# Lag products for two channels at once, both products of a table step in one instruction, and a new order: a gated mix of memory attention and a state-space convolution

## The chip, the cores and the metric

One core of one Trainium2 chip runs the whole program. Time is in device microseconds of that core. Before the change three runs gave 304.19, 305.31 and 306.17 us; the median is 305.31. Tables and prices below come from one profiled execution of the same kernel.

The engines are TensorE (PE, with its weight loads shown apart as PEld), VectorE (DVE), ScalarE (ACT), GpSimd (POOL) and SyncE (SP), which issues the DMAs.

## What is computed

A sequence x of 2048 tokens with 512 channels goes through two branches that a per-token gate mixes:

```python
g = sigmoid((x * gate_w).sum(-1, keepdims=True))
a = A_ref(x, wq, wk, wv, wo, beta)     # 32 heads of 16, 4 segments of 512 tokens
b = B_ref(x, A_re, A_im, B_re, B_im, C_re, C_im, log_dt, Dskip)
out = g * a + (1 - g) * b
```

Branch A is attention inside each segment (scores, causal mask, softmax, product with v) and, from the second segment on, a memory read: phi(q) times a matrix M, divided by phi(q) times z, where M and z gather phi(k) and v of the segments before. The two are mixed per head and projected with wo.

Branch B is a long convolution per channel d:

```python
dt = exp(log_dt)[:, None]
P  = exp((dt * A)[:, :, None] * l)           # d x 128 x l, l in bf16
K  = einsum('dn,dnl,dn->dl', C, P, dt * B).real
y  = irfft(rfft(pad(u)) * rfft(pad(K)))[:, :L] + u * Dskip
```

The lags l are rounded to bf16, so only some 640 distinct lags occur among the 2048. Each of them is a sum f + g of one of 20 exponents and one of 32. For one channel, K at all these lags is the real part of a product of two small complex matrices over n = 128: a table G of 32 entries (C times dt B, times a power) and a table F of 20 entries (powers of exp(dt A)).

## The kernel before, in words

The program is a graph of 1779 operations, built in Python by `build_graph`. Each has an engine (or may be done by ACT or DVE, for evacuations of PSUM), its operands and the tiles it needs. `ORDER` (line 370) is one long string with all the operations by number, in the order in which they enter their engines' queues: a suffix a or v puts an evacuation on ACT or DVE, and the numbers behind slashes name the buffers taken. `replay` reads it, `emit` (line 264) turns dependences into semaphore waits. On DVE and ACT these cover operations of the same engine too; on PE they do not. So within each engine the instructions run strictly as `ORDER` has them. The `cost` arguments and the `S.key` times belong to the search that made the string and do nothing on the chip.

The work falls into parts that overlap in time.

- Preparation (`ssm_prep`, line 754): six parameter matrices are transposed on PE two at a time (line 763) and evacuated (line 768); dt comes from a one-row matmul and an exponential on ACT (line 774); then sines, cosines and exponentials give exp(dt A). `ssm_powers` (line 816) squares it nine times, on ACT (826) and DVE (827, 828), and writes each power to a `pw` tile in bf16. `ssm_cb` makes C times dt B in `CBT` and a diagonal term.
- Attention: for 4 segments and 4 groups of 8 heads, projections, scores, one exponential of 128x2048 on ACT (line 1100, 80 in all), products with v, normalisation on DVE (lines 1072 to 1075), memory read, transpose to `oT`.
- Tables (`tables`, line 1169): for each of four blocks of 128 channels, 12 calls of `cmul` fill the tiles F and G. In a tile, the partition is n and the free index is channel pair, entry, channel within the pair; the real plane of 64 pairs comes first and the imaginary one behind it. A `cmul` step multiplies n entries by one power: a product with the real part, written in place (line 1197), a product with the imaginary part into a scratch tile `t2` (line 1200), and an addition of `t2` with its planes exchanged (line 1204).
- Lag products (line 1234): for each channel, the G table (32 columns, taken as PE's weights) times the F table (20 columns), first one plane, then the other. Four channels sit side by side in four column tiles of 32. A block takes 256 matmuls in 8 groups of 32, two evacuations of 320 columns into `kex`, and four DMAs that spread `kex` over the partitions of `KTT`.
- Convolution (`conv`, line 1251): x goes through a first transform (`x_level1`, line 876) and by way of DRAM (`scr_Z`); 32 steps transform K and x, multiply on DVE (line 1328), transform back and write `V2`. The constants `c_DN` are loaded step by step.
- The last part (`finals`) sums all into 16 output tiles and stores them.

F, G and the pool of `t2` (two buffers) lie at the same addresses as the buffers of the convolution's second half. In the trace nearly all matmuls carry one line (696, a helper), and evacuations carry lines 226 and 227 (ACT and DVE) or 229 and 230 (with a scale); DMAs carry line 222.

Of the kernel before, what the change touches and what calls it, by code (L numbers as in the profile page):

```python
# [98 lines left out]
class Sched:  # L99
# [45 lines left out]
    def ap(self, T, off=0, dims=None, p0=0, np_=128, n=None, dt=None, pstep=1):  # L145
        dt = dt or T.dt
        T = T.tile
        esz = 4 if dt == F32 else 2
        if T.isp:
            h = self.ps32 if dt == F32 else self.ps16  # L150
            base = T.slot * 2048 // esz
        else:
            h = self.sb32 if dt == F32 else self.sb16
            base = (T.pool.addr + T.slot * T.pool.size) // esz
        v = h[:]
        st = v.ap[0][0]
        if dims is None:
            dims = [[1, n]]
        return bass.AP(v.tensor, v.offset + p0 * st + base + off, [[pstep * st, np_]] + [list(d) for d in dims])

# [210 lines left out]
10/0 0/0 9/1 29/4/0 15/0 16/0 35/0/0 36 214/0 30v 45/0 46/1 27/0 198/0 37/2 38/3 40/4 44/5 41 47/6 63/0 66/1 42 48  # L371
64/2 39/7 51/0 13/2 43 53/8 49 50 14/3 67v/0 52/9 56/0 54/10 55 70/1 58/11 57/12 61/0 59/13 60 68/0 69 76/2 82/3
33/5/1 65a 83v/0 22/0 3/0 80/1 26/0 81 17/3 18 11/4 12/5 31/0/2 32v 199 62 94/4 23/0 71v/1 95v/2 92/2 93 209/1/0/0
210a 84 187/5 400/1 74/3 24/0 7/0 75 1/0 211 107v/3 72 106/6 221/2 182/7 223/0/0/0 96 386/0 34a 104/0 105 212/6/0 222a
262/7/1 215/1 185/1 213a 224 263a 108 118/1 188/2 186/0 86/3 116/0 808/0 217/2 73 1003v/0 225 200 85 1004v 97 117
190/1 87/0 249/0/0 216a 131v/4 218a 19 250 251 130/3 88 20 1223/1 226 259/1/1/1 128/0 183/3 260a 261 387/2 129 809/0
810/0 388 5/0 1244/0 142/4 109 1005v 184 228/0/1 229 132 264/1/1/1 230 597/0 140/0 141 143v/5 219/0 205/2 119a/6 154/5
237/0/2 238 120 265 266 1007a/0 1012/0 1011 1009/1 1006a 201/0 21 1013 403/1 152/3 239 206 153 8/0 164/0 1008 267
207/0 1224/3/0 1225a 220a 598/2 121 167v/7 1017 599 98/3 2/0 1010 232/0/3 233 1018/0 234 168 1014 1019 165/1 231/2 166
1015/1 302/3/2/2 155v/8 1226/0 133 1016 1020 100/7 176a/9 1227a 144 275/0/1 276 235 236 99 404a 202/0 1021/0 277 177  # L380
169 1026 1022 1027/1 303a 244/0 240 305/1/2 241/1 6/0 156 306a 245/0/3 1028 246 247 4/0 145 1024/0 1245/3/1 343/1/0/0
344a 1246a 208/0 189 242 110/0 304 1247/1 1248a 1023 178 1029 1228 1236/3/0 280/0/2 281 157 248 345 1249 1237a 282 252
1234/1 1030/1 1235a 1238 1032 1231/3/1 1025 1232a 253 243/0 271/0/3 272 273 346/1/0 1031 1229/3 1033/0 1230a 347a
292/0/0 1039/1 1034 1255/2/0 293 1256a 111/6 294 1233 1038 274/3 1239/1/1 254/2 112 255 1035 1257/2 278 1258a 1240a
288/0/3 289 279 290 389 1040 227/2/0 268 1241/1 1242a 256 283 284/3 307/0/0/0 308 390/0 269/0 1259 316/0/1 317 318
1042/0 1036/1 287/2 291 1243 1041 285 1265/1 257/1 258a/0 1043 122/3 295 296 329/0/2 310 330 1037 331 297/4 203 191
1044/1/0 309 123/3 1045 1046 298 124 286/1 1047 1048a 204 136/5 299 348/0/1/1 391/1 349 134/2 312/0/3 313 314 270 135
1049/1 350 1250/3/0 1251a 1050 1051 1052 1053a 1054/0 1057 1055 146/0 1252/2 1253a 333/0/0 334 335 1254 1062v/0 315/0
1061v/0 392/3/1/1 1059v 393a 1058v 1056 148/4 1060v 1283/1/1 1284a 1067/0 28/0 1066 319 320 1063 1064/1 1068 1065 1072
1260/2/0 1073/0 113v/1 1082/1 355/0/3 356 1074 452/3/1 114 147 311/1 351 352 1069 1075 115 357 89a/3 1076/0 1081  # L390
321/0/1 322 1077 453a 353 90 1261a 323 91 407/3 408a 158/1 1078 328/2 324 325/5 1083 326 409/1/0/0 410 411 1262/3
1263a 1085/0 359/0/1 360 1079/1 327/0 101a/0 102 361 1084 405/3 499/1/2/2 406a 332 500a 125a/6 1087 364/0/2 365 366
1080 192/0 193/0 126 401/3 336 337 1086 338/0 394 1286/0 1088/1 339 1281/1 1282a 1264 402a 1094/0 1089 372/0/0 373
1271/0/0 374 1272a 103 1093 137a/4 395/1/2 396a 358/3 362 340 363 376/0/3 377 371/0 127 378 367 1095 1273/2 1274a 1285
160/1 449/1/0/0 450a 414/0/1 1090 1091/1 415 1070/0 375 379 457/2/1/1 1275 416 458 1092 300/1 301a 368/1 1097/1 77a/7
1096 1071 418/0/2 369 419 1098 459 380 381/2 420 1104/1/1 149v/5 78 1105 159 79 501 451 1106 1107 138 139 382 383/1
161a/8 1268/2/1 431/0/0 173v/2 432 170/3 172/7 370 171 433 1108v 616/0/0 174 175 456/0 179v/9 1269a 1099/3 1100 1101
1102 1117a/0 1113a/0 435/0/3 1103a 617a 1111 1292/1/0 412 1116v 1115v 436 1293a 1114v 162 1118 1119/0 1122/1 502/2/0
1121 437 1120 163 1266/3 1294/0 417/1 1123 1128/0 180 421 1267a 1270 1124 1127 150 151 423/0/1 424 1137/1 460 503a
# [1077 lines left out]
```

## Time and profile before

| | us |
|---|---|
| median of three runs | 305.31 |
| the profiled execution, whole | 304.8 |
| its span, first to last instruction | 303.0 |
| first of the 80 score exponentials starts | 22.0 |
| last of them ends | 278.1 |
| products and additions of the tables (lines 1197 to 1204) | 28.9 to about 161 |
| busy time of lines 1197, 1200, 1204 | 33.6, 33.5, 32.5 |
| busy time of the 1024 lag matmuls | 10.1 |
| mean granted clock | 0.974 |

The 1.8 us between span and whole lie outside the instructions. Busy time of a group is the union of its instructions, and the mean of one, in ns, stands behind it. Instructions on DVE and ACT overlap: the next one starts before the last has ended, so the step from start to start is shorter than the duration. The chain of waits is followed back from the last instruction; a piece called issue is time in which an engine waited for nothing that the profile shows. A stretch's row gives each engine's busy time in it with the number of instructions.

### The profile page before, as it was taken

The numbers are of one execution on the slowest core, as the hardware profiler recorded it, in microseconds if no ns is written. First come the engines' busy times: TensorE is split into PE (matmuls) and PEld (weight loads), VectorE is DVE, ScalarE is ACT, GpSimd is POOL, SyncE is SP. The second block draws the span as 40 slices with busy tenths as digits, with TensorE's granted clock in tenths as the row PEclk, the third lists the DMA queues.
The fourth block names the chain that finished last, engine by engine and source line by source line (L and its number), as shares of the span: only waits on it lengthen the run. The fifth ranks groups of instructions, "written<-read, shape, count | busy, mean of one in ns | idle before, by whom it ended". The sixth has DMA issues, their size and how long they took to land.

```text
span 303.0 us, 9760 instructions
## 1 busy us (share of the span) xinstructions
PE 263.9 (87%) x4154; PEld 155.4 (51%) x4154; DVE 263.4 (87%) x630; ACT 262.8 (87%) x327; POOL 3.2 (1%) x9
## 2 busy tenths in 40 slices
PE   2798767787877979889997999989999999999993
PEld 1544435554554625575753666555545455545651
DVE  2999999999999899799997799999999998856182
ACT  2999999999998997999997999998889899888121
POOL 2000000000000000000000000000000000000000
PEclk9999999999988978999998999999999999999998
DMA  6989122322401333234520256676586665730234
GB/s 151 270 177 204 41 90 98 114 59 44 134 35 43 110 125 106 82 112 141 142 74 4 66 150 191 182 209 188 167 238 180 185 202 159 249 107 2 69 116 163
DMA packets 46589, 39.23 MB, mean 129 GB/s; under 512 B 21585, under 2 KB 42450, under 8 KB 46546
## 3 DMA queue, kind: packets, MB, share of 16 engines
q1 hardware_dynamic: 46546, 38.60, 45.1%
q8 instruction: 33, 0.54, 0.7%
q14 instruction: 10, 0.08, 0.1%
HBM read 20.37 MB, written 6.29 MB: 88 GB/s over the span
## 4 chain that ended last, share of the span: by engine, by line
PE 44%; DVE 27%; ACT 19%; issue 4%; DMA 3%; SPq 1%; DVEq 0%
PE psum L696 43%; ACT sb L1100 9%; DVE sb L1200 7%; DVE sb L1197 7%; DVE sb L1204 6%; ACT sb L226 5%; ACT sb L826 2%; DMA sb<-c_DN 2%; SPq L222 1%; DMA sb<-sb 1%; DMA sb<-in_B_A_re_dram 1%; DVE sb L1075 1%; DVE sb L1022 1%; DVE sb L1154 1%; DVE sb L1072 1%
## 5 line engine op out<-in xcount | busy, mean ns | idle before, releaser
L696 PE MATMUL psum<-sb 128*128 128x17 bf16 (+12 forms) x4066 | 258.0, 229 | 27.1 <-ACT sb L1100 12.7
L696 PEld LDWEIGHTS psum<-sb 128*128 128x128 bf16 (+4 forms) x4066 | 149.4, 96 | 133.3 <-ACT sb L1100 26.9
L1100 ACT ACTIVATE sb<-psum 128x2048 bf16<-128x2048 f32 x80 | 152.2, 1902 | 7.4 <-PE psum L696 6.8
L226 ACT ACTIVATE sb<-psum 128x512 bf16<-128x512 f32 (+3 forms) x156 | 86.0, 608 | 13.1 <-PE psum L696 12.7
L227 DVE CAST sb<-psum 128x512 bf16<-128x512 f32 (+2 forms) x58 | 35.9, 629 | 5.5 <-PE psum L696 4.9
L1197 DVE TENSOR_TENSOR sb<-sb 128x512 bf16<-128x512 bf16 (+3 forms) x48 | 33.6, 717 | 0.3 <-ACT sb L226 0.2
L1200 DVE TENSOR_TENSOR sb<-sb 128x512 bf16<-128x512 bf16 (+3 forms) x48 | 33.5, 712 | 0.1
L1204 DVE TENSOR_TENSOR sb<-sb 128x512 bf16<-128x512 bf16 (+3 forms) x48 | 32.5, 687 | 0.2
L1112 DVE TENSOR_TENSOR sb<-sb 128x1024 bf16<-128x1024 bf16 (+1 forms) x40 | 23.0, 577 | 3.5 <-ACT sb L1100 3.4
L1328 DVE TENSOR_TENSOR sb<-sb 128x1024 bf16<-128x1024 bf16 x32 | 21.7, 684 | 2.8 <-DMA sb<-sb 2.5
L229 ACT ACTIVATE sb<-psum,sb 128x512 f32<-128x512 f32 (+1 forms) x11 | 7.1, 685 | 9.1 <-PE psum L696 9.0
L1075 DVE TENSOR_TENSOR sb<-psum,sb 128x256 bf16<-128x256 f32 x32 | 13.4, 418 | 0.4
L1072 DVE RECIPROCAL sb<-psum 128x16 f32<-128x16 f32 x32 | 8.0, 252 | 4.8 <-PE psum L696 4.6
L826 ACT ACTIVATE sb<-sb 128x512 f32<-128x512 f32 x18 | 11.7, 658 | 0.0
L230 DVE TENSOR_SCALAR sb<-psum,sb 128x512 bf16<-128x512 f32 (+1 forms) x5 | 3.7, 748 | 6.4 <-PE psum L696 6.4
L1154 DVE TENSOR_TENSOR sb<-psum,sb 128x512 bf16<-128x512 f32 x12 | 8.2, 688 | 0.3
L1031 ACT ACTIVATE sb<-sb 128x512 bf16<-128x512 bf16 x12 | 7.6, 637 | 0.3 <-PE psum L696 0.3
L827 DVE TENSOR_TENSOR sb<-sb 128x256 f32<-128x256 f32 x18 | 7.6, 422 | 0.0
L980 ACT ACTIVATE sb<-psum 128x512 bf16<-128x512 bf16 x12 | 7.6, 634 | 0.0
L828 DVE SCALAR_TENSOR_TENSOR sb<-sb 128x256 f32<-128x256 f32 x18 | 7.4, 419 | 0.0
L1385 DVE SCALAR_TENSOR_TENSOR sb<-psum,sb 128x512 bf16<-128x512 f32 x8 | 5.6, 745 | 1.3 <-PE psum L696 1.2
L763 PE MATMUL psum<-sb 128*128 128x128 bf16 x24 | 2.7, 280 | 4.4 <-DMA sb<-in_B_A_re_dram 4.4
(70 smaller groups left out, 105.8 us busy)
## 6 DMA issues: line engine op xcount, KB each, us to landing
sb<-sb SPq DMA_DIRECT2D x64, 128.0 KB, 3.2
sb<-c_DN SPq DMA_DIRECT2D x32, 224.0 KB, 2.9
scr_Z<-sb SPq DMA_DIRECT2D x16, 256.0 KB, 2.1
sb<-scr_Z SPq DMA_DIRECT2D x16, 256.0 KB, 3.8
sb<-in_A_x_dram SPq DMA_DIRECT2D x5, 512.0 KB, 4.5
out_dram<-sb SPq DMA_DIRECT2D x8, 256.0 KB, 2.3
sb<-c_DN SPq DMA_DIRECT2D x12, 160.0 KB, 2.3
sb<-sb SPq DMA_DIRECT2D x20, 64.0 KB, 2.0
```

The lines of the kernel that those rows point to most:

```text
L226: fa = lambda e: e.activation(dst(), src(), ACT.Copy)
L227: fd = lambda e: e.tensor_copy(dst(), src())
L696: mm = lambda e, o_, l, r_, st, sp, **kw: e.matmul(o_, lhsT=l, rhs=r_, start=st, stop=sp, skip_group_check=True, **kw)
L826: op("ACT", ("As", 512), lambda e, sq=sq, Z=Z: e.activation(ap(sq, n=512), ap(Z, n=512), ACT.Square), r=[Z], w=[sq], key=PW[h] + PWS * k)
L1075: op("DVE", ("V1", 256), lambda e: e.tensor_tensor(ap(o1, gi * 16, [[128, 4], [32, 4], [1, 16]]), ap(T, dims=[[68, 4], [17, 4], [1, 16]]), ...
L1100: o = op("ACT", ("Ax", 2048), lambda e, P=P, pT=pT: e.activation(ap(pT, n=2048), ap(P, n=2048), ACT.Exp, scale=0.25), r=[P], w=[pT])
L1112: op("DVE", ("V2", 128 * nb), lambda e, pT=pT, dims=dims: e.tensor_tensor(ap(pT, dims=dims + [[1, 128]]), ap(pT, dims=dims + [[1, 128]]), ...
L1154: op("DVE", ("V1", 512), lambda e: e.tensor_tensor(ap(o2, 0, [[128, 4], [16, 8], [1, 16]]), ap(P2, 0, [[256, 4], [17, 8], [1, 16]]), ap(R2 ...
L1197: op("DVE", ("V2n1" if n == 1 else "V2", 256 * n), lambda e: e.tensor_tensor(run(tile, ne, dst, 1), run(tile, ne, src, sstep), ap(pw, cl * ...
L1200: op("DVE", ("V2n1" if n == 1 else "V2", 256 * n), lambda e: e.tensor_tensor(run(t2, n, 0, 1), run(tile, ne, src, sstep), ap(pw, cl * 512 ...
L1204: op("DVE", ("V2n1" if n == 1 else "V2", 256 * n), lambda e: e.tensor_tensor(D_(), D_(), ap(t2, n * 128, [[-n * 128, 2], [2 * n, 64], [1, ...
L1328: op("DVE", ("V2", 1024), lambda e, Y=Y, XAB=XAB, K3=K3, xo=xo: e.tensor_tensor(ap(Y, dims=[[512, 2], [1, 512]]), ap(XAB, xo, [[512, 2], [ ...
```

## The change

It has five parts.

1. F and G grow by spare entries behind the real ones: 4 for F (20 become 24) and 8 for G (32 become 40). The tile `t2` goes. A `cmul` step whose source entries are adjacent writes both products in one instruction with an outer dimension of two: real to the destination, imaginary to the spare entries. Three of the twelve steps of a table (sources 5, 2 and 2 entries apart) keep two instructions. The addition reads the spare entries. 27 instructions per table instead of 36.
2. A lag matmul takes a pair of channels: 64 weight columns (32 entries of each) by 40 columns (20 of each), in two column tiles of 64. Half of the 64 by 40 results mix the two channels and are not used. 128 matmuls per block, in 8 groups of 16; three evacuations (480, 480 and 320 columns) into a `kex` of twice the size with one buffer.
3. So that the right rows come out, channels are permuted: channel c and c + 32 of each 64 become neighbours. The parameter evacuations, the read of log_dt and the diagonal's matmuls (16 instead of 4) do this, and the four DMAs out of `kex` take every second partition.
4. The table pools take 12288 and 20480 bytes a partition for F and G (10240 and 16384 before) and nothing for `t2` (8192).
5. `ORDER` is another string throughout: 1747 operations, other places for nearly all, other engines for some evacuations, other buffers.

```diff
-    FP = mkpool("F", 10240, 1)
-    GP = mkpool("G", 16384, 1)
-    t2P = mkpool("t2", 4096, 2)
+    FP = mkpool("F", 12288, 1)
+    GP = mkpool("G", 20480, 1)
...
-    kexP = mkpool("kex", 1280, 2)
+    kexP = mkpool("kex", 2560, 1)
...
-            S.evac(lambda T=T: ap(T, n=1024), lambda P=P: ap(P, n=1024), 1024, r=[P], w=[T], psum16=True)
+            S.evac(lambda T=T: ap(T, 0, [[64, 16], [2, 32], [1, 2]]), lambda P=P: ap(P, 0, [[64, 16], [1, 32], [32, 2]]), 1024, r=[P], w=[T])
...
-                i = mm(e, ap(P, c, n=1), ap(CBT, 512 + c * 128, n=128), ap(onesT, n=1), True, True)
+                for q in range(4):
+                    i = mm(e, ap(P, c, n=1, p0=32 * q, np_=32), ap(CBT, 512 + c * 128 + 64 * (q // 2) + q % 2, [[2, 32]]), ap(onesT, n=1), True, True, tile_position=(0, 32 * q))
...
+        EF, EG = NF + 4, NG + 8
+        FPL, GPL = EF * 128, EG * 128
...
-            t2 = Tile(t2P, BF16)
-            run = lambda T, E, e0, st: ap(T, 2 * e0, [[2 * E, 128], [2 * st, n], [1, 2]])
-            op("DVE", ("V2n1" if n == 1 else "V2", 256 * n), lambda e: e.tensor_tensor(run(tile, ne, dst, 1), run(tile, ne, src, sstep),
-                                                                 ap(pw, cl * 512, [[2, 128], [0, n], [1, 2]]), ALU.mult),
-               r=rd + [pw], w=wr + [tile])
-            op("DVE", ("V2n1" if n == 1 else "V2", 256 * n), lambda e: e.tensor_tensor(run(t2, n, 0, 1), run(tile, ne, src, sstep),
-                                                                 ap(pw, cl * 512 + 256, [[2, 128], [0, n], [1, 2]]), ALU.mult),
-               r=rd + [pw], w=[t2])
+            if sstep == 1:
+                op("DVE", ("V2n1" if n == 1 else "V2", 512 * n), lambda e: e.tensor_tensor(
+                    ap(tile, 2 * dst, [[2 * (sp - dst), 2], [2 * ne, 128], [1, 2 * n]]), ap(tile, 2 * src, [[0, 2], [2 * ne, 128], [1, 2 * n]]),
+                    ap(pw, cl * 512, [[2, 256], [0, n], [1, 2]]), ALU.mult), r=rd + [pw], w=wr + spp + [tile])
+            else:
+                for half in range(2):
...
-                D_(), D_(), ap(t2, n * 128, [[-n * 128, 2], [2 * n, 64], [1, 2 * n]]), ALU.add), r=[t2], w=wr)
+                D_(), D_(), ap(tile, 2 * sp + ne * 128, [[-ne * 128, 2], [2 * ne, 64], [1, 2 * n]]), ALU.add), r=spp, w=wr)
...
-        for hf in range(2):
+        for b0, nb in ((0, 12), (12, 12), (24, 8)):
             P = S.ps()
...
-                            for dq in range(4):
-                                dl = 32 * dq + 16 * hf + sl
-                                i = mm(e, ap(P, sl * NF, n=NF, p0=32 * dq, np_=32), ap(G, (1 - cc) * GPL + (dl // 2) * 2 * NG + dl % 2, [[2, NG]]),
-                                       ap(F, cc * FPL + (dl // 2) * 2 * NF + dl % 2, [[2, NF]]), cc == 0, cc == 1, tile_position=(0, 32 * dq))
+                            for hh in range(2):
+                                dl = 64 * hh + 2 * (b0 + sl)
+                                i = mm(e, ap(P, sl * 40, n=40, p0=64 * hh, np_=64), ap(G, (1 - cc) * GPL + dl * EG, n=2 * NG),
+                                       ap(F, cc * FPL + dl * EF, n=2 * NF), cc == 0, cc == 1, tile_position=(0, 64 * hh))
...
-                  lambda dq=dq: ap(kex, n=640, p0=32 * dq, np_=32), 40960, r=[kex], pw=[KTp[c // 2]])
+                  lambda dq=dq: ap(kex, 640 * (dq % 2), n=640, p0=64 * (dq // 2) + dq % 2, np_=32, pstep=2), 40960, r=[kex], pw=[KTp[c // 2]])
```

More of the change, by code (lines that the diff above doesn't have):

```diff
@@ L159, in ap, with adr @@
         return bass.AP(v.tensor, v.offset + p0 * st + base + off, [[pstep * st, np_]] + [list(d) for d in dims])
+    def adr(self, T):
+        return (T.pool.addr + T.slot * T.pool.size) // 2
     def op(self, eng, cost, fn, r=(), w=(), pw=(), key=None, acq=(), alts=None, isdma=False, tr=False):
@@ L376 @@
[L376 to L385, printed above, removed]
@@ new lines @@
+735 772 1483/2 1482 1471v 1484/2 1485a 997/0 717/1 1371/4 1335/5/2 1360 764 802/3/4/0 1511/3 1546/0 1330/2 1372a 998
+746 747 1472/1 1473/4/0 1503 1467a 1336a 803 715/1 804 805 1331v 1367 748 1474a 749/5 736/0 750 751/0 1376 737
+1512/0/0 1513v 1514/2 794/0/0 869/2/0 870v 795 796 1547/3/1 1548a 738 873/0 790/0/1 1391/1 791 816 1515/0/2 1516v
+866/2/2/2 867v 1341 1518/1 789/3 1375 1549/3 955/1/1 1340 1486/0 1399/0 999/0 1000/0 956a 835/0/2 836 1532/3 1001
+1519/2/2 1487/0/3 792 793 1488v 716 1517 868 1550/1/2 871/0 872 1490/2 837 797 1520a 1521/1 798 799/1 800 1468 1525/0
@@ L459 @@
+1687/0 1688 1704 1666a 1705 1744/1 1739 1719/4 1727 1728/2 1720 1721 1740a 1729a 1745v 1746 1654/2 1655/3 1656 1732
+1733 1698a 1660/6 1680/3 1681 1661 1662 1722/4 1693/5 1694/5 1695 1734a 1735 1714/0 1663 1682 1689 1715 1716 1717
+1723a 1718v 1673/2 1674/1 1667/1 1668 1675 1724 1699/3 1700 1701 1702 1669 1676 1706/2 1708/6 1709 1710 1711 1712v
+1707a 1713
 """
```

181 lines of the change are left out of this document (92 added, 89 removed).

## The prediction

> **What bounds the kernel now.** I read the page's busy rows first. Columns: busy time, share of the span, instructions.
>
> ```profile
> PE 263.9 (87%) x4154; PEld 155.4 (51%) x4154; DVE 263.4 (87%) x630; ACT 262.8 (87%) x327; POOL 3.2 (1%) x9
> ...
> q8 instruction: 33, 0.54, 0.7%
> ```
>
> Three engines are equally busy, so the average names no bound. The second line is the queue that brings instructions: 33 blocks, 0.54 MB, so 16 KB each. Then I cut the span into stretches.
>
> ```profile
> 24.00:57.00 33.00, 24.32 (x363) 14.36 (x359) 32.97 (x84) 32.86 (x45) 0.00 (x0) 1.00 0.42 102
> 57.00:96.00 39.00, 32.63 (x875) 19.94 (x875) 38.65 (x101) 38.95 (x50) 0.68 (x1) 0.96 0.24 67
> 96.00:133.00 37.00, 31.83 (x633) 19.08 (x633) 33.31 (x78) 33.57 (x45) 0.00 (x0) 0.91 0.31 96
> ...
> 202.00:278.00 76.00, 74.97 (x864) 40.38 (x864) 64.75 (x146) 68.72 (x76) 0.00 (x0) 1.00 0.60 173
> 278.00:303.00 25.00, 19.77 (x166) 11.19 (x163) 11.05 (x20) 6.04 (x11) 0.00 (x0) 0.96 0.29 106
> ```
>
> Columns: PE, PEld, DVE, ACT, POOL busy, granted clock, DMA share, GB/s. From 24 to 96 us DVE and ACT are full and PE waits for them; this is where the tables lie. From 202 us PE is full and DVE has 11 us to spare. The middle belongs to nobody: all three lose time. The chain of waits says what happens there (start, us, what).
>
> ```profile
> 90.30 5.07 PE psum L696 x262
> 95.37 2.02 issue
> ...
> 161.34 1.50 PE psum L696 x136
> 162.84 1.78 issue
> ...
> 266.11 31.68 PE psum L696 x285
> ```
>
> Both "issue" pieces stand right behind a burst of lag matmuls: 256 of them between 90.3 and 95.1, 128 from 161.3. PE has nothing to wait for and yet does nothing. In the DMA records a block of queue q8 starts at 95.05 and takes 1.03 us, another at 162.45 and takes 0.95; each stall ends soon after such a block has landed. When PE is starved, blocks start 3.5 to 3.8 us apart (91.29, 95.05, 98.71). A matmul with its weight load is two instructions, 128 bytes, so the 1024 lag matmuls are 8 of the 33 blocks. I read the stalls as instruction supply. A half-clock window of 3.4 us follows the second one (164.3 to 167.8 in the clock records). Prices come from the groups by form and from successive starts on DVE.
>
> ```profile
> L696 PE MATMUL psum<-sb 128*128 128x17 bf16 x1280 | 43.5, 171 | 4.0 <-issue 1.8 <-ACT sb L1100 1.2 <-DVE sb L1204 0.7
> L1197 DVE TENSOR_TENSOR sb<-sb 128x2048 bf16<-128x2048 bf16 x12 | 14.7, 1222 | 0.0
> L696 PE MATMUL psum<-sb 128*32 128x20 bf16 x1024 | 10.1, 178 | 1.0 <-issue 0.5 <-DVE sb L1204 0.2 <-ACT sb L226 0.2
> ```
>
> ```profile
> 82.39 1.22 DVE L1204 TENSOR_TENSOR sb<-sb 128x2048 bf16<-128x2048 bf16 x1
> 83.52 0.42 DVE L1197 TENSOR_TENSOR sb<-sb 128x512 bf16<-128x512 bf16 x1
> 83.86 0.42 DVE L1075 TENSOR_TENSOR sb<-psum,sb 128x256 bf16<-128x256 f32 x1
> ```
>
> A DVE instruction of 1.22 us is followed by the next start after 1.13; one of 512 elements (0.42 us) after 0.34. What it costs the queue is the start-to-start step: (1.13 - 0.34) / 1536 = 0.51 ns an element and about 0.08 us fixed. With the lower-quartile step of each row the queues sum to 251.2 us on ACT and 257.7 on DVE. On PE the steps between starts are 0.216 us for 512 columns, 0.111 for 256, 0.056 for 128 and 0.025 for 17: 225 us in all.
>
> **The change part by part.** The profiled execution took 304.8 us for a span of 303.0; the median is 305.3, 0.5 more.
>
> *Merged products.* Nine of twelve steps per table write both products at once: 36 instructions fewer, the same elements. 36 x 0.08 = 2.9 us off DVE at most; merging one-element steps, whose rows run slower per element, may give nothing, so I take 2.1. The operands keep their two adjacent bf16 elements innermost, so I expect the same 0.51 ns an element. The add now reads the spare entries; it still waits for one earlier product. The spare entries serialise the steps of one table as its own products did, and t2's two buffers go. [...]
>
> [...]
>
> *Lag products on PE.* 1024 matmuls of 32 weights by 20 columns become 512 of 64 by 40. The row gives 10.1 us for 1024, 9.9 ns each, four column tiles side by side. Not shown is the 64-wide form. Bounds: 512 x 9.9 ns = 5.1 us below, and above 512 x 34 ns = 17.4 us (43.5 us over 1280 from the 17-column row, which has no tiles beside it). Two tiles instead of four, each with twice the columns: I take twice 9.9, so 10.1 us again and no change, since this form is nearest in kind to the tiled row. The ends are -5 and +7; most of that lies beside full DVE and ACT queues up to 173 us, so I count -2 to +4 of it.
>
> *Instruction supply.* 512 matmuls fewer are 1024 instructions, four blocks of the 33 (the diagonal adds 12 matmuls). In the new ORDER a table's lag groups are 128 matmuls, one block, where they were 256. The two stalls on the chain are 3.8 us, and a third one, of 0.5, lies inside the first table's burst, off the chain. I take two thirds of 3.8: -2.5, since DVE kept working through half of the first stall and is next in line. Bounds 0 and -4.3. The half-clock window behind the second stall costs up to half of 3.4 us; I take -0.8, bounds 0 and -1.7.
>
> [...]
>
> *Evacuations.* Lag: 8 of 320 columns (452 to 484 ns) become 8 of 480 and 4 of 320. Between the 320 form (0.452) and the 512 form (0.629) a 480 one takes 0.60: 8 x 0.60 + 4 x 0.46 = 6.6 us against 3.7, so +2.9 busy, ten of the twelve on ACT. The parameter evacuations read with a stride: on DVE the 0.69 us of 1024 bf16 columns may stay or become about 1.2, the rate of the f32 row (512 columns in 0.684); I take 1.2. The first one ended at 6.18 and DVE's next instruction waited for ACT's exponential until 6.73, so 0.55 us of wait covers it; if dt were earlier it would cost 0.5. The permuted read of log_dt and the 16 small matmuls of the diagonal (163 ns rows, side by side) lie beside DVE work: nothing.
>
> *kex and its DMAs.* One buffer instead of two: the next table's first lag matmul must wait for four DMAs of 2.2 us. Tables end some 30 us apart, so nothing; uncovered, 2.2 us plus the queue on SP. The DMAs stay 16 of 40 KB, but read every second partition; at twice the time they still land tens of microseconds before K uses them.
>
> *The order.* Every queue is moved, SP's loads too, so I add the steps that ORDER puts ahead of chosen points. Ahead of the 25th score exponential (103.7 us): ACT 92.1 to 91.6, DVE 96.5 to 94.7. Ahead of the 57th (202.2): ACT 180.6 to 179.5, DVE 185.7 to 186.2, PE 136.6 to 136.2. Left for PE behind it: 88.7 to 88.9. These sums hold the merges and evacuations above. In all ACT sheds 4.5 us and DVE takes 4.7, because net eight 512-column evacuations, most of them V and the spilled outputs, go over to DVE; that is after 181 us, under PE, with 11 us free. At the first exponential ACT has 2 us more ahead of it, made good by the ninth. I take -0.3 for the queues up to 202 us and 0 after; a new order also moves waits that no sum shows: 3 us either way.
>
> Sum: 304.8 - 0.3 - 2.5 - 0.8 + 0 = 301.2 for the profile, 301.7 with the median's 0.5.
>
> **The rivals.**
> *No gain from supply.* The stalls recur at other blocks (17-column matmuls at 34 ns also eat a block in 4.4 us) or were hidden behind DVE. Speaks for it: four bursts of 128 (57.8, 124.0, 130.1, 170.7) showed no stall, so a burst alone does not make one. Against: both long ones stand behind a burst. Then 304.8 - 0.3 + 0.5 = 305.0. [...]
>
> *The tail grows (other side).* After the last score exponential (ends 278.1) PE had 21.2 us of steps queued and ended 20.2 later. The new ORDER leaves 25.5. If that exponential ends no earlier, the end moves by 4.3 x 20.2 / 21.2 = 4.1: 309.4. It decides from an exponential ending after 274. ACT's queue ahead is 5.6 shorter and PE's 4.6, which speaks against; DVE's is 2.1 longer, and the new DVE evacuations stand there, which speaks for.
>
> [...]
>
> *More than the stalls.* The clock records show 13.7 us at half clock (89.3, 109.7, 164.3); without them and both stalls, 304.8 - 6.8 - 2.5 + 0.5 = 296.0.
>
> **How the numbers follow.** Forecast 0.50 (own range 297 to 304.5), no gain 0.20, tail 0.20, half rate 0.03, more 0.07. One per cent, about what a measurement tells apart, is 302.3 to 308.4. Faster: 0.36 of the forecast, 0.03 and 0.07, 0.46. Same: 0.14 + 0.15 + 0.04 = 0.33. Slower: 0.02 + 0.16 + 0.03 = 0.21. The range 296.5 to 309.5 takes in the tail and most of the best case.
>
> **What would show it.** Merges: twelve 4096-element products of about 2.3 us; 4.4 means half rate. Lag: 512 matmuls with busy about 10 us; 5 or 17 are the ends. Supply: 29 or 30 blocks on q8, and no issue piece of 1.5 us or more behind a lag burst in the chain. Tail: the last exponential at or before 274 us. Wrong it is if the issue pieces stay, or if the middle, 96 to 202 us, loses more to waits than the 12 us that DVE loses up to there now.

## The result and the profile after

Over 21 runs the changed kernel took 304.21 us in the median (302.69 to 307.47), the kernel before 305.48: a ratio of 0.9951, 95% interval [0.993, 0.9972]. Set beside each other once more on another chip they gave 0.9926 [0.9889, 0.9963]. So the change gains between a half and three quarters of a per cent, where the forecast was 1.2. The profiled execution took 303.26 us for a span of 301.5. Ratios and mean clocks leave out the executions that lie more than 1.5 per cent above the fastest of their kernel, where there were such (eight of the twelve of e3, below).

First the page's busy rows (busy time, share, instructions) and the instruction queue.

```profile
PE 263.7 (87%) x3654; PEld 154.3 (51%) x3654; DVE 269.8 (89%) x609; ACT 260.0 (86%) x316; POOL 3.2 (1%) x9
...
q8 instruction: 29, 0.48, 0.6%
```

PE's time has not changed although it issues 500 matmuls fewer, and q8 has lost the four blocks that the prediction counted. Next the same stretches as before; columns are PE, PEld, DVE, ACT, POOL busy, granted clock, DMA share, GB/s.

```profile
24.00:57.00 33.00, 25.39 (x320) 13.60 (x318) 31.91 (x73) 31.87 (x41) 0.00 (x0) 0.95 0.44 120
57.00:96.00 39.00, 31.32 (x545) 18.87 (x546) 38.97 (x89) 39.00 (x51) 0.66 (x1) 1.00 0.21 63
96.00:133.00 37.00, 31.62 (x640) 20.38 (x638) 34.94 (x78) 34.41 (x46) 0.00 (x0) 0.95 0.33 101
202.00:278.00 76.00, 75.68 (x874) 40.65 (x871) 68.70 (x154) 63.35 (x67) 0.00 (x0) 1.00 0.57 168
278.00:301.50 23.50, 18.18 (x128) 9.91 (x125) 10.45 (x17) 6.38 (x10) 0.00 (x0) 1.00 0.31 112
```

In the middle (96 to 133) DVE is busy for 1.6 us more of the 37 than before and ACT for 0.8 more, so both idle less there. From 24 to 57, where both had been full to 0.15 us, each now loses 1.1: that is new. The chain of waits (start, us, what) names some of it.

```profile
33.13 5.61 DMA sb<-in_A_x_dram
38.88 1.44 PE psum L696 x13
...
105.59 4.29 DMA scr_Z<-sb
110.61 4.08 PE psum L696 x16
...
164.03 2.06 PE psum L696 x100
166.11 1.88 ACT sb L1101
...
260.98 35.22 PE psum L696 x309
```

The issue pieces behind the lag bursts are gone: the fourth table's burst at 164.0 is followed at once by an exponential. Among the transfers that stand in the chain now, two are new waits in the middle of full work: a load of x that PE waits for at 38.9, and a store of the first transform that ACT waits for at 110. The last piece is the tail, now 35.2 us of PE.

How far each execution had come is best read at the score exponentials, in ACT's records of the trace (ends, in us; half clock is the time at half clock before 295 us, from the clock records):

| execution | 1st | 17th | 57th | 80th | span | half clock |
|---|---|---|---|---|---|---|
| before | 23.8 | 76.7 | 202.2 | 278.1 | 303.0 | 13.7 |
| after | 26.7 | 78.7 | 200.4 | 272.1 | 301.5 | 10.2 |
| after, second execution (e16) | 27.1 | 80.9 | 202.9 | 274.6 | 304.0 | 17.1 |
| x load early (e14) | 26.3 | 77.8 | 200.6 | 272.5 | 301.9 | 10.2 |
| no merges (e7) | 25.5 | 78.3 | 199.5 | 271.1 | 300.5 | 10.2 |
| SP reordered (e12) | 38.9 | 90.9 | 212.2 | 284.3 | 313.7 | 27.3 |
| old lag form, new order (e8) | 28.2 | 83.3 | 216.8 | 288.6 | 318.0 | 30.7 |
| the same, half its lag matmuls (e11) | 26.4 | 79.1 | 205.3 | 277.4 | 306.8 | 20.5 |
| before, half its lag matmuls (e10) | 23.8 | 77.4 | 199.2 | 276.6 | 301.5 | 20.5 |

The changed kernel ends its first exponential 3.0 us late, is 2.0 late at the 17th and 1.8 early at the 57th; from the 57th on PE is full, and 100.8 us remain in the kernel before and 101.1 in the changed one. The profiled execution of the changed kernel was a good one: e16 is 2.5 us longer, 2.2 of it by the 17th exponential.

### The profile page after: what moved, and what is told of

It reads as the page before. It is cut to its first block, busy times and chain, and to the rows that moved or that the text cites. A ratio compares the mean times of both kernels' runs of the same rounds, so it can differ in the third digit from the quotient of the medians.

```text
span 301.5 us, 8741 instructions
## 1 busy us (share of the span) xinstructions
PE 263.7 (87%) x3654; PEld 154.3 (51%) x3654; DVE 269.8 (89%) x609; ACT 260.0 (86%) x316; POOL 3.2 (1%) x9
## 4 chain that ended last, share of the span: by engine, by line
DVE 37%; PE 35%; ACT 13%; DMA 8%; SPq 3%; issue 1%; ACTq 0%
PE psum L696 35%; DVE sb L1199 12%; ACT sb L1101 8%; DVE sb L1208 8%; ACT sb L229 4%; DVE sb L1204 3%; SPq L225 3%; DMA sb<-in_A_wk_dram 2%; DMA sb<-sb 2%; DMA sb<-in_A_x_dram 2%; DVE sb L1076 2%; DVE sb L230 1%; DMA scr_Z<-sb 1%; DVE sb L827 1%; DVE sb L828 1%
## 5 line engine op out<-in xcount | busy, mean ns | idle before, releaser
L696 PE MATMUL psum<-sb 128*128 128x17 bf16 (+14 forms) x3566 | 259.1, 237 | 28.1 <-ACT sb L1101 12.1
L696 PEld LDWEIGHTS psum<-sb 128*128 128x128 bf16 (+5 forms) x3566 | 149.0, 99 | 135.5 <-ACT sb L1101 29.3
L229 ACT ACTIVATE sb<-psum 128x512 bf16<-128x512 f32 (+4 forms) x153 | 85.3, 607 | 13.6 <-PE psum L696 11.8
L1199 DVE TENSOR_TENSOR sb<-sb 128x1024 bf16<-128x1024 bf16 (+3 forms) x36 | 48.5, 1359 | 0.1
L230 DVE CAST sb<-psum 128x512 bf16<-128x512 f32 (+2 forms) x65 | 40.1, 628 | 3.8 <-PE psum L696 3.5
L1208 DVE TENSOR_TENSOR sb<-sb 128x512 bf16<-128x512 bf16 (+3 forms) x48 | 32.9, 703 | 0.1
L1204 DVE TENSOR_TENSOR sb<-sb 128x512 bf16<-128x512 bf16 (+1 forms) x24 | 14.9, 621 | 0.0
L1076 DVE TENSOR_TENSOR sb<-psum,sb 128x256 bf16<-128x256 f32 x32 | 13.4, 420 | 0.3
L232 ACT ACTIVATE sb<-psum,sb 128x512 bf16<-128x512 f32 (+1 forms) x8 | 5.4, 685 | 9.3 <-PE psum L696 9.3
L826 ACT ACTIVATE sb<-sb 128x512 f32<-128x512 f32 x18 | 11.8, 663 | 0.0
L233 DVE TENSOR_SCALAR sb<-psum,sb 128x512 f32<-128x512 f32 (+1 forms) x8 | 5.8, 736 | 1.8 <-PE psum L696 1.6
L230 DVE COPY sb<-psum 128x1024 bf16<-128x1024 bf16 x3 | 2.5, 865 | 4.2 <-PE psum L763 4.2
```

The lines of the kernel that those rows point to most:

```text
L229: fa = lambda e: e.activation(dst(), src(), ACT.Copy)
L230: fd = lambda e: e.tensor_copy(dst(), src())
L696: mm = lambda e, o_, l, r_, st, sp, **kw: e.matmul(o_, lhsT=l, rhs=r_, start=st, stop=sp, skip_group_check=True, **kw)
L826: op("ACT", ("As", 512), lambda e, sq=sq, Z=Z: e.activation(ap(sq, n=512), ap(Z, n=512), ACT.Square), r=[Z], w=[sq], key=PW[h] + PWS * k)
L1076: op("DVE", ("V1", 256), lambda e: e.tensor_tensor(ap(o1, gi * 16, [[128, 4], [32, 4], [1, 16]]), ap(T, dims=[[68, 4], [17, 4], [1, 16]]), ...
L1199: op("DVE", ("V2n1" if n == 1 else "V2", 512 * n), lambda e: e.tensor_tensor(ap(tile, 2 * dst, [[2 * (sp - dst), 2], [2 * ne, 128], [1, 2 ...
```

## The experiments

The theory after the result: the instruction supply is cured as forecast, and the new order takes part of the gain back at its start and in new waits. Rivals: that the supply is worth little, that the merges cost something, or that the lag products' PE time, not their number of instructions, is what counts. Every ratio below is against the kernel before on the same chip.

**Contents in the old order (e2, e3, e4).** The dependences of the new graph were kept and the sequence was taken from the kernel before, operation by operation: the whole change, the lag form alone, the merges alone.

```diff
 ORDER = """
-214/0 10/0 0/0 16/0 9/1 29/0/0 202/0 30v 15/0 35/1/0 36 45/0 38/1 27/0 37/2 198/0 199 46/3 39/4 51/0 17/4 40/5 13/2 18
+10/0 0/0 9/1 29/4/0 15/0 16/0 35/0/0 36 214/0 30v 45/0 46/1 27/0 198/0 37/2 38/3 40/4 44/5 41 47/6 63/0 66/1 42 48
...
```

> The whole change in tables, lag products and channel order, but with the operations in the order of the kernel before (a merged product stands where the first of the two stood). Theory S: the contents are worth the two stalls, 2.5 to 3.5 us, so 302 to 303, ratio 0.988 to 0.992. Rival R: the contents are worth little and the search found the half per cent, ratio 0.998 to 1.004. A third view: products and additions that now wait for each other cost DVE more than they save in an order that was not made for them, ratio above 1.004.

> The pair form of the lag products alone (with the channel order, the three evacuations and the one kex), separate products with t2 as before, in the order of the kernel before. Theory S: the stalls behind lag bursts go, ratio 0.988 to 0.993. Rival (the stalls were hidden beside DVE): no long issue piece in the chain but ratio 0.998 to 1.005, the evacuations costing what the stalls gave.

> The merged products alone, lag products of single channels as before, in the order of the kernel before. Theory S: the stalls stay, DVE saves 1 to 2 us in the tables, ratio 0.995 to 1.000. Rival (a product that writes the tile waits for the one before it, and the addition stands right behind its product): ratio 1.000 to 1.010, with the additions and unmerged products longer than 0.46 us per 512 elements.

Measured: whole change 1.0389 [1.0335, 1.0443]; lag form alone 1.0082 [1.0029, 1.0136]; merges alone 1.0186 [1.0116, 1.0256]. In the two with the pair form no wait for issue is longer than 0.8 us; with the merges alone the longest is 2.4. So the stalls follow the lag form, but none of the three contents gains in an order that was searched for other contents. (Their profiled executions also spend 27 to 34 us at half clock, against 13.7 before.) The table steps on DVE (start to start) take 98.1 us in the whole change and 97.0 with the merges alone, against 90.9 before. With the merges alone 2.2 of these 6.1 us lie in the steps themselves and 3.9 in longer waits behind them. Part of the first is this: 21 additions stand right behind a product, and 12 of them leave DVE idle for some 35 ns in front. Such a step from a 1024-element product takes 0.84 us in the median (four of them), where it takes 0.70 with another instruction behind it. In the changed kernel's trace four additions leave DVE idle so.

**The start's order (e1).** The first 189 operations in the order of before, the rest as changed.

> The changed kernel, with the first 189 operations (up to the third score exponential, SP's loads among them) in the order of the kernel before. Theory S (the new order starts 3.0 us late, and that costs the end): first exponential ends at 23.8 instead of 26.7 us and the time falls to 301.0 to 302.3, ratio 0.985 to 0.990 to the kernel before. Rival R (the late start is absorbed by full queues later): first exponential earlier all the same, time within 0.7 us of the changed kernel, ratio 0.993 to 0.998.

Measured: 1.0183 [1.0142, 1.0225]. The first exponential ended at 23.7, as meant, but a hole opened between 30 and 48 us, where ACT waits 3.9 us for stores of the first transform and DVE is busy for only 8.6 us of the 18; the clock was at half from 37 to 54 us besides. The splice made its own trouble, so this run says nothing on the late start.

**Loads first (e5).** Fourteen operations moved: the weight loads ahead of x's first load, its first matmuls behind the first projections.

```diff
-11/3 12/4 63/0 31/2/1 200 19 20 21 41 14/5 42 43 64/3 53/6 44/7 47/8 48 1/0 26/0 52/9 56/0 54/10 32a 55 68/0 33/1/2 49
+11/3 12/4 63/0 23/0 31/2/1 200 19 20 21 41 14/5 22/0 42 43 64/3 53/6 44/7 47/8 48 1/0 26/0 52/9 56/0 54/10 32a 55 68/0
...
```

> The changed kernel with 14 operations moved near its beginning: the loads of wk, wq and wv and of the score mask go ahead of the first 512 KB load and the constants of the first convolution level, whose three first matmuls and evacuations go behind the first projections. All else stays. Theory S (late start costs the end): first score exponential ends at 24 to 25 instead of 26.7 us and the ratio to the kernel before falls from 0.995 to 0.986 to 0.990. Rival R (the start is absorbed before 60 us by full DVE and ACT queues): the exponential comes earlier, the ratio stays at 0.993 to 0.998.

Measured: 0.995 [0.992, 0.998], first exponential at 26.6. The loads' order is not what holds the start: in the changed kernel ACT has worked 20.6 us by the end of the first exponential, where it had worked 18.3.

**The merges (e6, e7).** In e6 the two products of an unmerged step no longer depend on each other; e7 has no merged product at all, with the changed kernel's order and lag form.

```diff
-                        ap(pw, cl * 512 + 256 * half, [[2, 128], [0, n], [1, 2]]), ALU.mult), r=rd + [pw], w=(spp if half else wr) + [tile])
+                        ap(pw, cl * 512 + 256 * half, [[2, 128], [0, n], [1, 2]]), ALU.mult), r=rd + [pw], w=(spp if half else wr + [tile]))
```

> The changed kernel, same order, with one dependence taken away: the second product of the three unmerged steps no longer counts as a writer of the whole tile, so it no longer waits for the first (they write different entries). If the waits between dependent DVE instructions ate the merges' gain, the unmerged products fall from 0.54 to about 0.46 us per 512 elements, DVE saves 1 to 1.5 us in the tables and the ratio falls by 0.002 to 0.005 to 0.990 to 0.993. If DVE was not on the path there: 0.995.

> The changed kernel in its own order, with the merges undone: separate products and t2 again, each pair standing where the merged one stood; the pair form of the lag products stays. Theory S, by the starts on DVE (0.08 us a merge): ratio 1.000 to 1.004, about 1.5 to 3 us over the changed kernel. Rival: the dependences of the merged form cost what it saves, ratio 0.993 to 0.998 as for the changed kernel.

Measured: e6 0.9948 [0.9906, 0.999], e7 0.9975 [0.9937, 1.0012]; the table steps take 89.9 and 89.8 us, with the merges 90.0. The merges are worth nothing that these runs can tell, though the intervals of e7 and of its neighbours on the same chip (e5, e6) are too wide to exclude 2 us. The groups by form show part of the reason: first two rows of the changed kernel, then one of e7.

```profile
L1199 DVE TENSOR_TENSOR sb<-sb 128x4096 bf16<-128x4096 bf16 x12 | 27.4, 2287 | 0.0
...
L1208 DVE TENSOR_TENSOR sb<-sb 128x512 bf16<-128x512 bf16 x20 | 9.3, 463 | 0.0
```

```profile
L1209 DVE TENSOR_TENSOR sb<-sb 128x512 bf16<-128x512 bf16 x20 | 8.4, 418 | 0.0
```

The large merged product keeps the full rate (2287 ns for 4096 elements, where 2048 took 1222 in the kernel before), and its step is 2.202 us where two single ones took 2 x 1.135: 0.068 saved, twelve times. But the additions of 512 elements take 463 ns in place of 418 when they read the spare entries, twenty times. I set the steps of the changed kernel beside those of e7, one by one, since both have the same order. The merged products save 1.3 us in all, 1.2 of it in the twenty largest and 0.1 in the sixteen smaller ones. The additions of 512 elements lose 0.8, and the 512-element products that stayed single lose 0.7. The sum is nothing. Why the single products lose is open: without their dependence (e6) 0.2 of the 0.7 comes back.

**The old lag form in the new order, whole and halved (e8, e11).** e8 has the merges and the changed order with the single-channel lag form (two evacuations, two kex buffers); e11 is e8 with 512 of its 1024 lag matmuls.

```diff
-        for b0, nb in ((0, 12), (12, 12), (24, 8)):
+        for hf in range(2):
...
-                        for cc in range(2):
+                        for cc in range(1):
                             for dq in range(4):
```

> The changed kernel in its own order, with the lag products of single channels again (1024 matmuls, two evacuations, the old channel order); the merges stay. Theory S (instruction supply costs PE some 3 us on the path): issue pieces of 1.5 us and more come back behind the lag bursts and the ratio rises to 1.002 to 1.008. Rival (the stalls are hidden): the pieces come back but the ratio stays below 1.000.

> The merged products with the old single form of the lag products in the changed kernel's order (the run that stood at 1.043), with the second plane's lag matmuls left out: 512 instead of 1024, each of 32 weights by 20 columns. Instruction supply: the five stalls of 1.1 to 2.3 us go, and the ratio falls by 0.035 or more, to 0.990 to 1.005. Rival, that the 4.8 per cent came from the old form's two evacuations and its place in this order: ratio stays at 1.03 or above.

Measured: e8 1.0434 [1.0393, 1.0475], e11 0.9998 [0.995, 1.0046]. Waits in all of the trace (engine, waited for, us in total, times, longest), first e8, then e11:

```profile
PEld psum L692 <- issue: 34.4, 102, 2.4
...
PE psum L692 <- issue: 10.5, 11, 2.3
```

```profile
PEld psum L692 <- issue: 23.0, 93, 0.4
...
PE psum L692 <- issue: 1.0, 6, 0.2
```

And three pieces of e8's chain:

```profile
63.21 1.99 PE psum L692 x206
65.20 2.16 issue
...
136.79 2.33 issue
...
179.21 2.25 issue
```

The same stalls as before, now five between 1.1 and 2.3 us instead of two, each at a lag burst; with half the instructions they are gone and 4.4% with them. The five make up 9.6 of these 13 us; the rest goes with 4.9 us less PE work and 10 us less at half clock, which this pair of runs does not separate. In the new order a table's lag groups stand back to back, so the old form hurts more there than in the old order. At most blocks nothing stalls: at the 29 of the changed kernel neither PE nor PEld waits longer than 0.5 us for issue, and at the 33 of the kernel before PE waits three times (0.51, 2.02 and 1.78 us). But the long stalls stand behind bursts of 128 to 256 matmuls of about 10 ns, and there the time fell by 1 to 4 per cent when half of the matmuls went.

**Half the lag matmuls in the kernel before and in the changed one (e10, e15).** The same cut, in the two kernels themselves.

```diff
-                        for cc in range(2):
+                        for cc in range(1):
```

> The kernel before in its own order, with the second plane's lag matmuls left out (512 of the 1024; so K lacks half of each product). Instruction supply as the prediction priced it: 29 blocks on q8, no issue piece of 1.5 us or more in the chain, and 2.5 to 4.3 us less, a ratio of 0.986 to 0.992. Rival, that in this order the stalls cost the end little because DVE and ACT lose the time again further on: stalls gone all the same, ratio 0.995 to 1.003.

> The changed kernel with the second plane's lag matmuls left out: 256 pair matmuls instead of 512, 27 blocks on q8, 4.8 us less PE work in the tables. If the 1.3 per cent that the same cut gave in the kernel before was instruction supply, nothing is left to gain here: 0.992 to 0.997. If it was the PE work of the lag products, the same again: 0.980 to 0.987.

Measured: e10 0.9866 [0.9811, 0.9922]; e15 0.9944 [0.99, 0.9989]. All waits for issue, before and then e10:

```profile
PEld psum L696 <- issue: 25.4, 85, 2.3
...
PE psum L696 <- issue: 4.3, 3, 2.0
```

```profile
PEld psum L696 <- issue: 20.8, 84, 0.4
...
PE psum L696 <- issue: 0.9, 4, 0.2
```

In the order of before the cut is worth 1.3%, and it gains nothing where no long stall is left, though it takes as much PE work away (the lag row's busy time falls from 10.1 to 5.8 us in e10, and from 10.8 in e16 to 6.4 in e15). That speaks for supply and against the rival of the PE time. It does not exclude a share of PE time in the 1.3%, as the chain before runs through the two bursts themselves (5.07 us at 90.3, 1.50 at 161.3). (An issue piece of 1.75 us that e10's chain has at 81.45 is no stall: an exponential runs on ACT from 81.43.)

**Twice as many narrow matmuls (e9).** Each pair matmul as two of 64 weights by 20 columns.

```diff
-                            for hh in range(2):
+                            for hh, h in ((0, 0), (1, 0), (0, 20), (1, 20)):
...
-                                       ap(F, cc * FPL + dl * EF, n=2 * NF), cc == 0, cc == 1, tile_position=(0, 64 * hh))
+                                       ap(F, cc * FPL + dl * EF + h, n=NF), cc == 0, cc == 1, tile_position=(0, 64 * hh))
```

> The changed kernel, each lag matmul of 64 weights by 40 columns issued as two of 64 by 20 (1024 again, same columns in all, same results, same evacuations and order). Instruction supply: 1024 instructions more are four blocks more on q8 (33), issue stalls of 1.5 us or more come back behind the lag bursts, and the time goes to 1.015 to 1.045 of the kernel before (the old single form in this order stood at 1.043). Rival, that the pair form wins by its shape, its three evacuations or its single kex: stalls stay away and the ratio stays at 0.992 to 0.998, as 20480 columns cost PE the same either way (busy 9 to 11 us).

Measured: 1.034 [1.0264, 1.0415]; against the expectation this form changes K's sums, so only its time counts here. q8 has 33 blocks again, but the longest wait for issue is 1.1 us. The row of the group tells what went wrong with the test:

```profile
L696 PE MATMUL psum<-sb 128*64 128x20 bf16 x1024 | 21.4, 187 | 3.2 <-issue 2.6 <-DVE sb L1208 0.5
```

1024 matmuls of 20 columns take 21.4 us, 512 of 40 took 9.6: 20.9 and 18.8 ns each. Nearly a third of the former ran at half clock; at full clock they start 16.1 ns apart in the mean inside a burst, and the changed kernel's 16.4. Half the columns cost the same, so PE got 11.8 us more work and the supply had more time. Inconclusive for the supply, and a price worth knowing (below).

**SP's queue by readiness (e12).** 33 issues moved: stores of the first transform and shifted copies of the powers right behind their last producer in the order, one load of x earlier.

```diff
-1195a 72 94/4 183/2 92/3 93 59/13 60/0 23/0 259/6/0/0 95v/2 260a 261 1193a 209/7/1/1 106/5 104/0 210a 61 22/0 212/0/0
+1195a 72 73 94/4 183/2 92/3 93 59/13 60/0 23/0 259/6/0/0 95v/2 260a 261 1193a 1196 209/7/1/1 106/5 104/0 210a 61 22/0
...
```

> The changed kernel with 33 of SP's issues moved: the stores of the first transform and the shifted copies of the powers stand right behind their last producer in the order, and the second segment's transposed load of x stands 55 places earlier. Theory that new waits behind DMAs in a reordered SP queue ate part of the gain: the 1.1 us wait of PE for x at 38.9 and the 1.6 us wait of ACT for a store at 110 go, and the time falls by another 0.8 to 2 us, a ratio of 0.988 to 0.992. Rival, that DVE and ACT are full there and the waits are made good in a few us: 0.993 to 0.997.

Measured: 1.0292 [1.024, 1.0343], a miss on both sides. SP's timeline (start, us, queue, line, what) tells it, first of the changed kernel, then of e12:

```profile
7.83 0.45 SPq L225 DMA_DIRECT2D sb<-in_A_wk_dram  x1
```

```profile
15.07 0.71 SPq L225 DMA_DIRECT2D sb<-sb  x1
15.82 0.61 SPq L225 DMA_DIRECT2D sb<-in_A_wk_dram  x1
```

A copy of a power (operation 73) now stands ahead of the load of wk (23) and waits until 15.07 for DVE; all loads behind it wait too. The first exponential ends 12.2 us late. And the table above shows what became of that: 12.2 at the 17th, 11.8 at the 57th, 12.2 at the last, 12.2 in the span. A little of this is the clock: e12 has a half-clock window of 10.2 us from 67.7 that the profiled execution of the changed kernel lacks. Against e16, which has one too, it is 11.9 at the first exponential and 9.8 in the span, and the ratios (1.0292 against 0.9926 and 0.9951) say 10 to 11 us. So time that ACT and DVE stand idle at the start is carried to the end for four fifths or more.

**One load, and three copies (e13, e14), beside the change itself (e16, e17).** The transposed load of x for the second segment (386) 21 places earlier; in e14 three of the second table's copies out of kex also behind a store.

```diff
-1007v/0 132 97 598/0 1011 599 121 1217 220a 153/5 1004v 1012 1005v 218a 2/0 221/3 222a 1196 1015 232/0/3 233 234 231/0
-208/0 1008 1207/1/0 1016 133 386/0 156 1209/2 1210a 1208a 1211 1017 1199/3/1 275/0/1 154 276 1200a 1197/2 1198a 1018
+1007v/0 132 97 598/0 1011 599 121 386/0 1217 220a 153/5 1004v 1012 1005v 218a 2/0 221/3 222a 1196 1015 232/0/3 233 234
+231/0 208/0 1008 1207/1/0 1016 133 156 1209/2 1210a 1208a 1211 1017 1199/3/1 275/0/1 154 276 1200a 1197/2 1198a 1018
```

> The changed kernel with one transposed load of x (second segment) 22 places earlier on the queue: ahead of a store that waited for an evacuation until 31.0 us, so issued at about 29.3 instead of 33.1. New waits in the order ate the gain: PE's wait of 1.1 us at 38.9 and DVE's of 1.0 at 40.3 go, nothing makes them good (a late start was carried through to the end in the run before), and the time falls by 0.5 to 1.1 us: 0.991 to 0.994. Rival, that another wait takes its place within some us: 0.994 to 0.997.

> As the run with the early load, and three of the second table's four spread copies of kex moved behind the first transform's last but one store, so that ACT's wait for a store at 108.3 to 110.0 us has fewer packets beside it. New waits: another 0.5 to 1.6 us less, 0.987 to 0.992. Rival: the wait stays (the store itself is issued only at 105.6, when its evacuation ends), same as the early load alone.

> The changed kernel itself, beside the early load on the same chip. If the early load's half per cent is its own: 0.993 to 0.997 here against 0.988 to 0.992 there. If it was the chip of that call: the two within 0.003 of each other.

> The changed kernel with the second segment's transposed load of x 22 places earlier, beside the changed kernel on the same chip. If the wait of 1.0 us that it removes counts: 0.3 to 0.5 per cent below the changed kernel. If another wait takes its place by the 29th exponential, as the traces suggest: the two within 0.003.

Measured: e13 0.9898 [0.9858, 0.9938] and e14 0.9904 [0.9865, 0.9943] on one chip; on another, side by side, the changed kernel (e16) 0.9926 [0.9889, 0.9963] and the early load (e17) 0.9918 [0.988, 0.9957]. So the early load gains nothing that can be told. Waits of the changed kernel from 28 to 57 us and from 92 to 135, then of e14 from 92 to 135:

```profile
PE psum L696 <- DMA sb<-in_A_x_dram: 1.1, 1, 1.1
```

```profile
ACT sb L229 <- DMA scr_Z<-sb: 1.6, 1, 1.6
```

```profile
ACT sb L229 <- DMA scr_Z<-sb: 1.9, 1, 1.9
```

In e14 the wait for x is gone, and ACT's idle time up to the ninth exponential is 0.6 us less (6.6 against 7.2); by the 29th it is 10.4 against 9.7. The store's wait grew, and the half-clock windows fell elsewhere. No version of the changed kernel tried here beats it beyond its interval.

## Why the prediction was wrong, step by step

**Merged products: mis-sized, by about the whole term.** Taken at -2.1, measured -0.9 in the table steps and +0.1 against e7 in the same order. The fixed 0.08 us was right for the large products (0.068); the prediction gave the small ones "may give nothing" and left the additions and the single products at their old price, and these lose as much as the others save. Half rate (4.4 us for a large merged product) is excluded by the 2287 ns.

**Lag products on PE: the right figure, in part by luck.** 9.6 us against 10.1 taken. I reasoned with columns (half the tiles, twice the columns). e9 shows that columns do not count at this size: at full clock its 20-column matmuls start 16.1 ns apart and the changed kernel's 40-column ones 16.4, both with two tiles of 64 side by side. With four tiles of 32 the step is 7.8, and in the 17-column row without tiles 25.4. So the price falls with the number of tiles side by side; as the weights are 64, 32 and 128 columns wide in these three, no run tells the number of tiles from the width of the weights.

**Instruction supply: right, in mechanism and size.** 29 blocks, and no issue piece over 0.33 us in the chain. The four blocks of 16 KB that went for 500 matmuls fewer are 131 bytes a matmul with its weight load, where 128 were taken. Taken at -2.5 and, with the clock, -3.3 (1.1%); e10 measured -1.3% [-1.9, -0.8], with some PE work gone besides. In the kernel before ACT waits for PE right behind each of the two stalls:

```profile
98.14 0.60 ACT L226 ACTIVATE sb<-psum 128x512 bf16<-128x512 f32 x1 [1.30 <-PE psum L696]
...
165.42 0.60 ACT L226 ACTIVATE sb<-psum 128x512 bf16<-128x512 f32 x1 [1.97 <-PE psum L696]
```

These 3.3 us are gone in the changed kernel. What makes one burst stall and not another stays open. The 256 matmuls that the prediction counts ahead of the first stall are two bursts of 128, from 90.3 and from 93.8; the second stall stands behind a single burst of 128, and other bursts of that size show none.

**The clock: not shown.** I took -0.8 for the window behind the second stall. That window is gone, others came. Over 90 executions of the kernel before the mean clock was 0.973, over 29 of the changed kernel 0.974. The windows differ from one execution to the next of the same kernel. Two of the changed kernel from 57 to 72 us (columns as in the stretches above), the first the one shown so far, the second e16:

```profile
57.00:72.00 15.00, 11.93 (x279) 8.01 (x278) 15.00 (x40) 15.00 (x20) 0.00 (x0) 1.00 0.21 61
```

```profile
57.00:72.00 15.00, 14.14 (x259) 10.21 (x261) 13.79 (x37) 13.68 (x20) 0.00 (x0) 0.66 0.15 41
```

A window of 10.2 us at half clock over the first lag burst, in the second, costs DVE and ACT 1.2 to 1.3 us. A window of that length starts between 57 and 60 us in the traces of e5, e13, e15 and e17 as well, and not in the one trace of the kernel before; so the profiled execution of the changed kernel is on the lucky side there.

**Evacuations and kex: right.** A 480-column evacuation took 0.593 us (0.60 taken), the strided one on DVE 1.23 (1.2). The lag matmuls' row shows no wait for a DMA, only 1.2 us for the last addition:

```profile
L696 PE MATMUL psum<-sb 128*64 128x40 bf16 x512 | 9.6, 187 | 1.2 <-DVE sb L1208 1.2
```

**The order: this step failed.** I took -0.3 for the queues up to 202 us, and 0 for waits that no sum shows. I worked out what each engine does up to the end of an exponential (time less idle time, from the trace's records):

| up to exponential | ACT idle, before / after | ACT at work | DVE idle | DVE at work |
|---|---|---|---|---|
| 1st | 5.5 / 6.1 | 18.3 / 20.6 | 5.9 / 6.3 | 17.8 / 20.4 |
| 9th | 5.5 / 7.2 | 45.5 / 46.5 | 6.0 / 7.4 | 45.1 / 46.4 |
| 21st | 5.6 / 7.2 | 83.1 / 83.1 | 6.2 / 7.4 | 82.5 / 83.0 |
| 25th | 7.0 / 7.2 | 96.7 / 96.9 | 7.4 / 7.4 | 96.4 / 96.7 |
| 29th | 8.8 / 9.7 | 109.9 / 109.7 | 7.4 / 9.3 | 111.3 / 110.0 |
| 45th | 12.3 / 10.5 | 155.6 / 157.5 | 13.4 / 9.7 | 154.4 / 158.3 |
| 57th | 13.9 / 11.7 | 188.3 / 188.7 | 14.3 / 11.3 | 187.8 / 189.1 |

ACT lost 13.9 us up to the 57th exponential and now loses 11.7. The 2.2 are 4.6 saved, 3.3 of them at the two stalls and 1.3 at other waits, less 2.4 that are new: 0.6 ahead of the first exponential, 1.1 from there to the ninth, where the load of x is, and 0.7 more from the 25th to the 29th, where the store is. ACT's work did not fall by 1.1 as the queue sums said but grew by 0.4, and DVE's grew by 1.2 instead of 0.5. So -4.6 + 2.4 + 0.4 = -1.8 at the 57th, and from there PE's work carries it to -1.5 at the end. In e16 the new waits are 4.4 in place of 2.4, some 1.2 of them in the half-clock window, and ACT has lost 14.1 us by the 57th, as much as before the change. "2 us more ahead of it, made good by the ninth" is half right: the 2.3 us of extra work are 1.0 at the ninth and gone by the 21st, as work done early must be. The idle time that came with it is not, as e12 shows for a larger stretch.

**The tail: right.** The last exponential ended at 272.1, ahead of the 274 from which the rival would decide, and PE ended 24.1 us later; 25.5 had been counted. (In the kernel before the records give 19.7 where the prediction has 20.2, which changes nothing.)

So the mechanism of the supply stands. The step that failed is the order, waits and queues together: taken at -0.3, and by ACT's account about +1.5 up to the 57th exponential (2.4 of new waits and 0.4 of work, less 1.3 of other waits that went), and more in e16. It took back about half of the 3.3 us that the stalls gave. The prediction allowed 3 us either way for "waits that no sum shows" and entered nothing for them in the sum. Its signs of being wrong do not show this: the issue pieces are gone, and from 96 to 202 us DVE is idle for 3.9 us, where it was for 8.1, while most of the new waits lie ahead of 57 us, where nothing was watched. No run isolates the order: this is where the idle time lies, and what remains beside the stalls (e10), the merges (e7) and PE's lag work (e15). It stays open why the windows at half clock fall where they do, and how much of the new waits another search of the order could remove; the load of x was moved, three copies were moved to shorten the wait for the store, and no gain in time can be told.

## What to carry to other kernels

When many tiny matmuls stand back to back, count instructions as well as PE time: half of them gone was worth up to 1.3% here and up to 4.4% in an order that packs them closer. Price a new order by the idle time it adds ahead of the first full stretch, since most of that is carried to the end (in e12 four fifths or more of 12.2 us), and not by work done early, which comes back (here 2.3 us, gone by the 21st exponential). Measure a change of contents in an order made for it: in the old order the parts of this one lose 0.8 and 1.9%, and the whole loses 3.9.

## What the runs showed of the hardware

- A matmul of 20 or 40 columns with its own weights costs the same with two tiles of 64 side by side: at full clock the next one starts 16.1 or 16.4 ns later (e9, the changed kernel). With four tiles of 32 and 20 columns it is 7.8, without tiles and with 17 columns 25.4.
- The same 512-element addition on DVE takes 418 ns with one layout of its second operand and 463 with another, where the 1024-element one stays at 682 to 684.
- From one execution of the kernel before to the next, the span goes with the mean clock: 1.1 us less for each 0.01 more, with a correlation of -0.69 over 90 executions on three chips. A difference of half a per cent is no larger than the scatter of single executions (1.4 us, one standard deviation).
